# Batch 0's decays apart from the other batches', in a re-ordered Mamba-2 and low-rank-mixer kernel

## The chip, the cores and the metric

The kernel runs on one core of one Trainium2 chip. The metric is the device time of one execution in microseconds (us). Runs of the same kernel differ by about 1%: the three runs of the kernel before took 219.33, 219.85 and 221.1 us.

## What is computed

Two blocks, one behind the other. The first is a chunked state-space scan (Mamba-2 SSD) with batch 4, 8 heads, sequence 768, head dimension 32 and state dimension 16; the second is a low-rank token mixer with a channel MLP on the 256 joined channels.

```python
# first block: x (4,8,768,32), a (4,8,768), B and C (4,8,768,16)
log_a = np.log(np.clip(a, 1e-06, 1.0))
for c in range(nc):                       # chunks of 32 steps
    cum = np.cumsum(la, axis=-1)
    L = np.exp(cum[:, :, :, None] - cum[:, :, None, :]) * causal
    y_intra = ((C B^T) * L) x
    y_inter = (C state) * exp(cum)
    state = exp(sum(la)) * state + sum_j B_j x_j exp(cum[-1] - cum_j)
# second block: x (4,768,256) from the first, U (768,32), V (32,768)
h = x.transpose(0, 2, 1) @ U @ V
u = x + h.transpose(0, 2, 1)
out = u + np.maximum(u @ w_ch1, 0.0) @ w_ch2     # w_ch1 (256,1024), w_ch2 (1024,256)
```

The weights U, V, w_ch1 and w_ch2 arrive as 64-bit floats. The kernel loads them as pairs of 32-bit words and builds single-precision numbers from them on the chip.

## The kernel before

The scan works on chunks of 64 steps. A batch has 768 steps, which are three "pairs" of two blocks of 128 steps, so there are twelve pairs, k = 0 to 11, three for each batch. The kernel is written as small steps, and one long string, PLAN (lines 41 to 75), lists every step in the order in which it is issued. `follow` (line 937) reads the words of the list one by one; there is no scheduler behind it. Each engine (TensorE is PE, VectorE is DVE, ScalarE is ACT, GpSimd is POOL, SyncE is SP) works off its own share of the list in that order, and waits where an operand or a buffer is not ready. Two more strings give each product its PSUM bank (BANKS) and each temporary its place in memory (SLOTS).

At the start, outside of the list, `a` is loaded, turned by two PE products (line 358), clamped by one DVE operation for all four batches (line 360) and put through the logarithm by one ACT operation (line 364). A product of ones (`ahead`, line 312) stands on PE before and after the turning, only to keep PE at work.

The words of the list that matter here; a digit behind the letter is the pair, or the batch:

- `A` (`decays`, line 384): products of the logarithms with a fixed matrix, then ACT's exponential into F; the word's number says whether the factors of B (0) or of C (1) are made. `K` (`keep`, line 403): three products, DVE's `own` and its reduction, ACT's exponential and a POOL product give the decays that carry the state from chunk to chunk (`kept`, `own2`). Before the change, both are for all four batches at once.
- `YX`, `YB`, `YU`, `YV`, `X`, `B`, `w`: loads on SP's queue, x as `x`, B and C as `bc`, and the weights as `words`. `X`, `B` and `w` without a Y are held until the DVE operation last listed is done (`hold`, line 202). `w0` and `w1` bring the first quarter of w_ch1 in two halves, `w2` to `w4` the other three, `w5` to `w8` the quarters of w_ch2.
- `Q` and `P` (`prep`, line 481): DVE multiplies B and C by the factors F into `BC`. `V` and `T` (`turn`, line 520): PE transposes BC, ACT or DVE copies it to `T` and `Cm`.
- `g` (`gram`): 32 products for C B^T; `m` and `M` (`mask`, line 549): DVE applies the causal mask into `M`. `n` and `j` (`intra`, line 676): each half of the intra-chunk products; `j` waits for a small POOL copy (`settled`, line 617), which waits for the products of `n`. `s` (`state`): products for the states, `u` (`update`): DVE's chain of states S, then POOL's product `Sm`. `i` (`inter`): products with the carried state.
- `y`, `t`, `O`: ACT copies the result of a pair out of PSUM, PE transposes it into token order (`ytok`).
- `p`, `q`, `a` (`project`, `parted`, `added`, from line 742): the low-rank mixer. `v` (`spread`, line 893): Vs is made from V. `c`, `C` (`convert`) and `R` (`refined`): the conversion of weights, in three steps over DVE, ACT and POOL, and their split into parts for the fast product form.
- `U` and `d0.0` (`plain`, `down`): the MLP of the first half of batch 0 in full single precision; `S`, `f`, `h`, `d`: the MLP of everything else, from split operands.
- `E` (`warm`, line 349) is a fill: PE multiplies the identity by itself, n blocks of 128 columns in one product, into a bank that nobody reads. It computes nothing.

Of the kernel before, what the change touches and what calls it, by code (L numbers as in the profile page):

```python
# [14 lines left out]
WCOLS = 512  # L15
PLAIN = 1
BANKS = (
    '01720345670012367400561273334612337423057406175233406175234061752304237562137054713054762167'
    '2305417351473512603512476305143051247626241762405761357204615304712530471240653206127346126731'
    '26705706254317062705647031520312304504153761021072016325040375403')  # L20
SLOTS = (
    'abcdefghijklmnocaefbdgihmecjbldkagofhimncjekandeblmneogmfcmhjiakdbnolefhmgcadjnbeilofkhjcmdeal'
    'gibfonmkjeclhbagfidnkomlej')


NEAR = 1.0 - 2.0 ** -13
# [3 lines left out]
AF = mybir.ActivationFunctionType  # L30
ALU = mybir.AluOpType
# [7 lines left out]


PLAN = (
# [34 lines left out]


@with_exitstack
def kernel(
# [27 lines left out]
    nc = tc.nc  # L107
# [249 lines left out]
    for g in range(2):  # L357
        nc.tensor.transpose(out=la_ps[:, g], in_=a_sb[:, g], identity=ident[:R, :R])
    ahead(80)
    vector.tensor_scalar(  # L360
        out=la.rearrange("p b c h -> p b h c"),
        in0=la_ps.rearrange("p g (b h c) -> p (g b) h c", h=NH, c=NC),
        scalar1=1e-6, scalar2=1.0, op0=ALU.max, op1=ALU.min)
    nc.scalar.activation(la, la, AF.Ln)

    middle = const.tile([P, P], FP32)
    vector.tensor_tensor(out=middle, in0=low[1], in1=low[0], op=ALU.subtract)
# [16 lines left out]
    def decays(bs, tag="w", which=range(2)):  # L384

        n = bs.stop - bs.start
        for i in which:
            d = bank(tag, n * NPR * NH * 2)
            view = d.rearrange("p (g h c) -> p c g h", g=n * NPR, h=NH)
            logs = la[:, bs].rearrange("p b (q c) h -> p c (b q) h", q=NPR)  # L390
            if i == 0:
                nc.tensor.matmul(out=view, lhsT=ref, rhs=logs, start=True, stop=True,
                                 skip_group_check=True)
            for c in range(2 if i else 0):
                for t in range(2):
                    nc.tensor.matmul(
                        out=view[ts(c, H), t], lhsT=ref.rearrange("p (i t) -> p t i", t=2)[:, t],
                        rhs=logs[:, c], start=t == 0, stop=True, skip_group_check=True)
            nc.scalar.activation(
                F[:, bs, :, :, i].rearrange("p b q h c -> p (b q h) c"),  # L400
                d.rearrange("p (g c) -> p g c", c=2), AF.Exp, scale=(-1.0, 1.0)[i])
# [485 lines left out]
    def convert(c, scalar=False):  # L887

        if c not in steps:
            steps[c] = to_fp32(*weights[c], c - 2 - NQ, scalar)  # L890
        next(steps[c])
# [33 lines left out]
    def ytokens_of(k, v):  # L925
# [4 lines left out]
                 j=lambda k: intra(k, 1), y=yout, t=ytokens, Q=lambda k, c: prep(k, c, 1),  # L930
                 O=ytokens_of,
                 V=lambda k, c, v: turn(k, c, 1, "wx"[v // 2], vector if v % 2 else None))
    whole = dict(c=convert, b=lambda c: convert(c, True), C=lambda n: convert(-1), R=refined, A=lambda i: decays(every_batch, "w", [i]),
                 K=lambda n: keep(every_batch, "z"), F=fill, E=warm,
                 v=lambda n: spread())

    def follow(plan):
# [54 lines left out]
```

## Time and profile before

| | before |
|---|---|
| median of three runs | 219.85 us (219.33 to 221.1) |
| the profiled execution, its own time | 221.66 us |
| its span, first to last instruction | 219.9 us |
| mean granted TensorE clock | 0.977 |
| PE busy | 211.3 us |
| DVE, ACT, POOL busy | 150.1, 87.6, 35.4 us |
| moved by DMA | 14.58 MB |

The profile is one execution, with every instruction's start and length on each engine. "Busy" is the time in which an engine had at least one instruction in work. For PE the ends are modelled, and consecutive products overlap. A row of the timeline gives the start, the time from the first start to the last end of a group, the engine, the source line, the operation, output and inputs, the shape and the count, and in brackets the idle time ahead of it with the instruction that ended it. A single-precision product is recorded as two passes, a transpose as one. Line 182 stands for all DVE operations, since a helper records them. SPq rows are the issuing of loads and stores; the data land later. "PEclk" is the share of full speed that the clock throttle granted to PE.

### The profile page before, as it was taken

The numbers are of one execution on the slowest core, as the hardware profiler recorded it, in microseconds if no ns is written. First come the engines' busy times: TensorE is split into PE (matmuls) and PEld (weight loads), VectorE is DVE, ScalarE is ACT, GpSimd is POOL, SyncE is SP. The second block draws the span as 40 slices with busy tenths as digits, with TensorE's granted clock in tenths as the row PEclk, the third lists the DMA queues.
The fourth block names the chain that finished last, engine by engine and source line by source line (L and its number), as shares of the span: only waits on it lengthen the run. The fifth ranks groups of instructions, "written<-read, shape, count | busy, mean of one in ns | idle before, by whom it ended". The sixth has DMA issues, their size and how long they took to land.

```text
span 219.9 us, 7021 instructions
## 1 busy us (share of the span) xinstructions
PE 211.3 (96%) x3058; PEld 186.8 (85%) x3058; DVE 150.1 (68%) x314; ACT 87.6 (40%) x196; POOL 35.4 (16%) x52
## 2 busy tenths in 40 slices
PE   7879989998999999999999999999999999999994
PEld 3646756666778989999999988999999999999993
DVE  4737796787768899789653779746518776647532
ACT  2342736567574555443053531236342222323000
POOL 3011023368570740001000101200000000000000
PEclk9965999999999999999999999999999999999999
DMA  5989584678686850203210301000000000100012
GB/s 94 107 121 133 121 139 110 143 217 216 135 117 118 132 62 3 48 16 82 29 51 3 72 3 48 30 3 1 3 0 24 30 23 0 48 16 11 0 53 93
DMA packets 69663, 14.58 MB, mean 66 GB/s; under 512 B 63808, under 2 KB 67840, under 8 KB 69632
## 3 DMA queue, kind: packets, MB, share of 16 engines
q1 hardware_dynamic: 69488, 14.06, 32.6%
q8 instruction: 24, 0.39, 0.8%
q10 hardware_dynamic: 144, 0.07, 0.1%
q14 instruction: 7, 0.06, 0.1%
HBM read 10.98 MB, written 3.15 MB: 64 GB/s over the span
## 4 chain that ended last, share of the span: by engine, by line
PE 86%; DVE 6%; SPq 3%; DMA 1%; issue 1%; POOL 1%; DVEq 0%; POOLq 0%
PE x L809 38%; PE z L809 27%; PE y L694 4%; SPq L210 3%; PE y L658 3%; PE x L544 2%; PE w L504 2%; DVE words L182 2%; PE w L721 2%; PE w L140 2%; DMA bc<-in_C_dram 1%; PE w L578 1%; DVE M L182 1%; DVE S L182 1%; PE w L747 1%
## 5 line engine op out<-in xcount | busy, mean ns | idle before, releaser
L182 DVE SCALAR_TENSOR_TENSOR words<-words 128x768 fp32r<-128x768 f32 (+3 forms) x39 | 35.9, 919 | 5.1 <-PE z L809 3.4
L809 PE MATMUL x<-w,words 128*128 128x256 f32 x224 | 34.4, 284 | 0.0
L809 PE MATMUL x<-u,w 128*128 128x384 f32 x168 | 33.9, 340 | 0.0
L809 PE MATMUL z<-u,w 128*128 128x384 f32 x168 | 33.0, 340 | 0.0
L833 ACT ACTIVATE words<-x 128x384 fp32r<-128x384 f32 x28 | 13.8, 492 | 44.0 <-PE x L809 43.9
L809 PEld LDWEIGHTS x<-w,words 128*128 128x128 f32 x224 | 30.5, 190 | 0.2 <-issue 0.2
L809 PEld LDWEIGHTS z<-u,w 128*128 128x128 f32 x168 | 29.1, 188 | 0.3
L809 PEld LDWEIGHTS x<-u,w 128*128 128x128 f32 x168 | 28.8, 188 | 0.4 <-issue 0.2
L809 PE MATMUL x<-w2c,words 128*128 128x256 f32 x144 | 25.2, 305 | 0.0
L833 ACT ACTIVATE words<-z 128x384 fp32r<-128x384 f32 x28 | 13.7, 491 | 25.3 <-PE z L809 25.3
L809 PEld LDWEIGHTS x<-w2c,words 128*128 128x128 f32 x144 | 21.1, 189 | 1.1 <-issue 0.4
L182 DVE SCALAR_TENSOR_TENSOR words<-z,words 128x384 fp32r<-128x384 f32 x28 | 15.4, 551 | 9.0 <-ACT words L833 8.9
L809 PE MATMUL z<-w,words 128*128 128x256 f32 x112 | 18.4, 287 | 0.0
L182 DVE SCALAR_TENSOR_TENSOR words<-x,words 128x384 fp32r<-128x384 f32 x28 | 14.9, 551 | 4.0 <-ACT words L833 3.8
L605 POOL TENSOR_TENSOR Sm<-S,own 128x256 f32<-128x256 f32 (+1 forms) x12 | 7.2, 602 | 61.6 <-DVE S L182 61.6
L809 PEld LDWEIGHTS z<-w,words 128*128 128x128 f32 x112 | 15.7, 190 | 0.2
L694 PEld LDWEIGHTS y<-M,x 64*32 64x32 f32 x768 | 8.7, 113 | 5.9 <-POOL settled L617 2.8
L694 PE MATMUL y<-M,x 64*32 64x64 f32 x768 | 12.0, 237 | 1.5 <-POOL settled L617 1.3
L809 PE MATMUL z<-w2c,words 128*128 128x256 f32 x72 | 13.2, 307 | 0.0
L182 DVE SCALAR_TENSOR_TENSOR S<-S,kept,w 128x64 f32<-128x64 f32 x40 | 11.2, 280 | 2.6 <-PE w L504 0.5
L182 DVE TENSOR_TENSOR M<-x,causal 128x256 int32<-128x256 int32 x24 | 9.0, 416 | 5.7 <-PE z L544 4.3
L182 DVE SCALAR_TENSOR_TENSOR ytok<-x,ytok 128x256 f32<-128x256 f32 (+1 forms) x17 | 6.8, 407 | 7.3 <-PE x L809 7.3
(137 smaller groups left out, 337.3 us busy)
## 6 DMA issues: line engine op xcount, KB each, us to landing
words<-in_moe_w_ch_dram SPq DMA_DIRECT2D x7, 512.0 KB, 5.3
x<-in_x_dram SPq DMA_DIRECT2D x24, 128.0 KB, 3.2
out_dram<-ytok SPq DMA_DIRECT2D x23, 128.0 KB, 1.7
bc<-in_B_dram SPq DMA_DIRECT2D x24, 64.0 KB, 3.2
bc<-in_C_dram SPq DMA_DIRECT2D x12, 128.0 KB, 3.3
words<-in_moe_w_ch_dram SPq DMA_DIRECT2D x2, 256.0 KB, 3.0
words<-in_moe_U_dram SPq DMA_DIRECT2D x1, 192.0 KB, 3.5
words<-in_moe_V_dram SPq DMA_DIRECT2D x4, 48.0 KB, 2.5
```

The lines of the kernel that those rows point to most:

```text
L140: nc.tensor.matmul(out=t[:, :m * P].rearrange("p (m i) -> p m i", i=P), lhsT=ident, rhs=ident[:, None, :].to_broadcast([P, m, P]), start=T ...
L182: self.last = call(*args, **kwargs)
L210: op = issuer[0].dma_start(**kwargs)
L504: nc.tensor.transpose(out=tp[:, i, v], in_=s["BC"][:, i, c + v].rearrange("p h n -> p (h n)"), identity=ident)
L544: nc.tensor.matmul(out=s["g"][r][cols, c], lhsT=s["T"][rows, 0, c, cols], rhs=s["Cm"][rows, :, :, ts(2 * c + p, Q)].rearrange("r v t i -> ...
L578: nc.tensor.matmul(out=s["A"][p][ts(r, Q), v], lhsT=s["BC"][half, 0, v, 2 * r:2 * r + 2].rearrange("p h n -> p (h n)"), rhs=x_sb[k][half, ...
L605: nc.gpsimd.tensor_tensor(out=s["Sm"][:, sl], in0=s["S"][:, sl].rearrange("p i (s d) -> p i s d", s=2), in1=own2[:, b, 4 * q + sl.start:4 ...
L658: nc.tensor.matmul(out=channels(k)[r // 2][ts(r % 2, H), c, p], lhsT=own[ts(r, Q)], rhs=st[k]["T"][ts(r, Q), 1, :, ts(2 * c + p, Q)].rearr ...
L694: product = nc.tensor.matmul(out=y[n][ts(i, Q), c, p], lhsT=x_sb[k][half, c, h], rhs=s["M"][half, h // 2, c, h % 2], start=fresh(k, n, [i] ...
L721: nc.tensor.transpose(out=t[:, c, g], in_=yT[b][:, g, ts(2 * q + c, P)], identity=ident)
L809: nc.tensor.matmul(out=t, lhsT=lhsT, rhs=rhs, start=start, stop=True, skip_group_check=True)
L833: nc.scalar.activation(gs[j, m // 2][0][:, m % 2], t, AF.Relu, scale=NEAR)
```

## The change

Behind the turning of `a`, the clamp is made twice, for batch 0 and for the other three; the logarithm of batch 0 follows at once, that of the others is a word of the list (`L0`). `A` now has four words, 0 and 1 for batch 0, 2 and 3 for the others, and `K` two. F, `kept` and `own2` are written by parts; their values are the same.

The list has a new order from the first word to the last, and so have BANKS and SLOTS. The first words are shown below up to the first products of the MLP; behind them the same words follow in another order. Fills before: E1, E2, E1, E1, E2, E1 (eight blocks, the first two words `E1` and `E2` ahead of the first intra products). After: E4 as the very first word, ahead of the decays, then E2, E4, E2 (twelve blocks).

```diff
-    vector.tensor_scalar(
-        out=la.rearrange("p b c h -> p b h c"),
-        in0=la_ps.rearrange("p g (b h c) -> p (g b) h c", h=NH, c=NC),
-        scalar1=1e-6, scalar2=1.0, op0=ALU.max, op1=ALU.min)
-    nc.scalar.activation(la, la, AF.Ln)
+    first, rest = slice(0, 1), slice(1, NB)
+    for bs in (first, rest):
+        vector.tensor_scalar(
+            out=la[:, bs].rearrange("p b c h -> p b h c"),
+            in0=la_ps.rearrange("p g (b h c) -> p (g b) h c", h=NH, c=NC)[:, bs],
+            scalar1=1e-6, scalar2=1.0, op0=ALU.max, op1=ALU.min)
+
+    def logs(bs):
+
+        nc.scalar.activation(la[:, bs], la[:, bs], AF.Ln)
+
+    logs(first)
...
-    whole = dict(c=convert, b=lambda c: convert(c, True), C=lambda n: convert(-1), R=refined, A=lambda i: decays(every_batch, "w", [i]),
-                 K=lambda n: keep(every_batch, "z"), F=fill, E=warm,
+    whole = dict(c=convert, b=lambda c: convert(c, True), C=lambda n: convert(-1), R=refined, L=lambda n: logs(rest),
+                 A=lambda i: decays((first, rest)[i // 2], "w", [i % 2]),
+                 K=lambda n: keep((first, rest)[n], "z"), F=fill, E=warm,
...
 PLAN = (
-    'YX0 A0 YB0 Q0.0 YB1 A1 Q0.2 Q0.1 K0 s0 YB2 YB3 Q1.0 V0.0.0 V0.1.1 Q1.2 YU0 YX1 Q1.1 u0 '
-    'Q2.0 E1 Q2.2 g0 m0 V1.0.2 B5 M0 V1.1.2 w0 V2.0.2 E2 n0 j0 g1 YX2 YV0 m1 i0 E1 P3 E1 M1 Q2.1 c0 '
-    's1 n1 u1 c0 T3 T3 E2 V2.1.3 c1 P5 j1 y0 i1 g2 m2 w1 O0.0 s2 c1 B4 y1 T5 u2 M2 T5 g3 C0 m3 i2 '
-    'n2 E1 X3 c0 j2 M3 y2 C0 c2 t1 C0 w3 c2 O2.1 v0 p0 s3 P4 T4 u3 X4 q0 c2 w2 T4 g5 a0.0 M5 X5 c4 '
-    'w5 m5 n3 c1 U0.0.1 U0.0.0 j3 g4 i3 c4 w6 c4 y3 m4 c3 s4 U0.0.4 R0 t3 U0.0.5 c3 c3 R1 u4 a0.1 '
-    'B6 U0.0.3 M4 c6 i4 w4 n5 c6 R0 n4 w7 c6 s5 U0.0.2 j4 j5 u5 y4 i5 c7 c7 y5 t4 d0.0.1.0 R4 t5 '
+    'E4 L0 A1 YX0 A0 YB0 Q0.0 YB1 YX1 Q0.2 Q0.1 V0.0.0 Q1.0 YU0 V0.1.1 K0 Q1.1 A2 s0 g0 Q1.2 YB2 '
+    'YV0 m0 V1.0.2 M0 V1.1.2 A3 n0 j0 YX2 g1 u0 Q2.0 m1 YB3 K1 B5 i0 y0 M1 s1 n1 c0 w0 X3 E2 w1 '
+    'Q2.2 C0 Q2.1 O0.0 j1 V2.0.2 s2 u1 E4 V2.1.3 i1 y1 u2 P3 g2 m2 M2 t1 P5 T3 T3 i2 c1 n2 C0 j2 g3 '
+    'E2 m3 c0 w3 C0 y2 O2.1 c0 v0 p0 M3 c2 c2 c1 B4 s3 c2 n3 u3 q0 T5 T5 a0.0 c1 w2 c4 c4 R0 j3 '
+    'a0.1 w4 U0.0.1 U0.0.0 P4 X4 g5 i3 c3 w5 c4 T4 y3 w6 U0.0.4 X5 c3 M5 T4 U0.0.5 m5 c5 c3 R0 '
+    'U0.0.3 t3 R2 c5 c5 s4 u4 c6 g4 U0.0.2 w7 c6 m4 M4 U0.0.6 c6 U0.0.7 c7 i4 c7 R2 c7 R1 d0.0.1.0 '
...
```

More of the change, by code (lines that the diff above doesn't have):

```diff
@@ L17 @@
 BANKS = (
-    '01720345670012367400561273334612337423057406175233406175234061752304237562137054713054762167'
-    '2305417351473512603512476305143051247626241762405761357204615304712530471240653206127346126731'
-    '26705706254317062705647031520312304504153761021072016325040375403')
+    '0120203456712035462034562714570062300146035271436005271403652714032714023765021743650215074362'
+    '2615643132015647013014756201362017453625254364152734620153470623470562503465036403267015430145'
+    '6726701453762145376521037634737437437142630750736506412547342453')
 SLOTS = (
-    'abcdefghijklmnocaefbdgihmecjbldkagofhimncjekandeblmneogmfcmhjiakdbnolefhmgcadjnbeilofkhjcmdeal'
-    'gibfonmkjeclhbagfidnkomlej')
+    'abcdefghijklmnodabgcefihladjgmifnkclbadhojecdhjmfjgnmbknbiloaecdgfhmnkjliboakcgejdhflnmcobieja'
+    'gndkfhmliocbjenaghdmkofjic')
 NEAR = 1.0 - 2.0 ** -13
```

56 rows, old and new, of the table PLAN are left out of this document.

## The prediction

> **What bounds the kernel now.** I read the cores' spans first, then the page's busy table and chain by engine, then a table of stretches, and last the timeline, engine by engine, up to the first product of the mixer.
>
> ```profile
> core 0: 219.9 us, clock 0.977
> PE 211.3 (96%) x3058; PEld 186.8 (85%) x3058; DVE 150.1 (68%) x314; ACT 87.6 (40%) x196; POOL 35.4 (16%) x52
> PE 86%; DVE 6%; SPq 3%; DMA 1%; issue 1%; POOL 1%; DVEq 0%; POOLq 0%
> ```
>
> PE holds 86% of the chain that ended last. Its products are nearly the same before and after, so the change can only win where PE waits or runs slowly. The stretches say where (columns: length, then busy time of PE, PEld, DVE, ACT, POOL, then granted clock, DMA share, GB/s):
>
> ```profile
> 9.28:12.69 3.41, 2.23 (x39) 1.36 (x40) 2.84 (x10) 2.36 (x10) 0.62 (x1) 1.00 0.93 113
> 12.69:16.10 3.41, 2.98 (x98) 1.86 (x102) 0.76 (x3) 0.75 (x3) 0.18 (x1) 0.50 0.75 121
> 16.10:19.52 3.42, 3.30 (x101) 2.60 (x88) 2.62 (x9) 0.38 (x1) 0.00 (x0) 0.50 0.83 118
> 19.52:22.93 3.41, 3.35 (x69) 2.13 (x55) 1.63 (x7) 1.33 (x3) 0.79 (x2) 0.50 1.13 175
> 29.76:33.17 3.41, 2.75 (x48) 1.32 (x49) 2.96 (x9) 1.99 (x7) 0.73 (x1) 1.00 0.78 160
> 70.00:80.00 10.00, 10.00 (x166) 9.42 (x164) 9.24 (x19) 5.30 (x11) 5.84 (x6) 1.00 0.82 120
> 80.00:100.00 20.00, 20.00 (x224) 19.62 (x201) 17.63 (x34) 9.22 (x19) 0.89 (x2) 1.00 0.14 29
> ```
>
> From 70 us PE is full. The loss lies in the first 37 us, and 10.24 us of it (12.69 to 22.93) ran at half clock, after a stretch in which PE was busy 2.23 of 3.41 us. These PE rows carry the rest:
>
> ```profile
> 2.13 1.06 PE L315 MATMUL x<-ones 128*128 128x512 f32 x1
> 4.51 1.01 PE L392 MATMUL w<-la,ref 128*128 128x192 f32 x2
> 9.60 0.35 PE L544 MATMUL x<-Cm,T 32*64 32x128 f32 x2 [0.89 <-DVE BC L182]
> 10.33 0.66 PE L504 MATMUL x<-ident,BC 128*128 128x128 f32 x4
> 12.51 1.08 PE L140 MATMUL w<-ident 128*128 128x256 f32 x2
> 13.64 0.68 PE L694 MATMUL y<-M,x 64*32 64x64 f32 x32
> 14.70 0.68 PE L694 MATMUL y<-M,x 64*32 64x64 f32 x32 [0.37 <-POOL settled L617]
> 15.31 0.48 PE L544 MATMUL x<-Cm,T 32*64 32x128 f32 x2
> 17.04 1.65 PE L140 MATMUL w<-ident 128*128 128x128 f32 x4
> 18.74 0.68 PE L578 MATMUL w<-x,BC 64*32 64x64 f32 x32
> 19.88 1.11 PE L504 MATMUL w<-ident,BC 128*128 128x128 f32 x4
> 20.79 1.06 PE L140 MATMUL w<-ident 128*128 128x256 f32 x2
> 22.53 0.61 PE L694 MATMUL y<-M,x 64*32 64x64 f32 x32
> 29.18 0.46 PE L694 MATMUL y<-M,x 64*32 64x64 f32 x32
> 31.53 0.35 PE L901 MATMUL y<-Vn,ident 32*32 32x192 f32 x2 [0.52 <-ACT Vn L895]
> 37.18 1.53 PE L809 MATMUL z<-yT,w1f 128*128 128x384 f32 x4
> ```
>
> The same four transposes cost 0.66 at full clock and 1.11 at half; 32 intra products 0.46 and 0.68. PE was busy 3.30 of 3.42 us in 16.10:19.52 and the clock still did not return, while 19.52:22.93 (3.35) brought it back. What differs is work on the whole 128x128 array: 1.65 of fills in the first; 1.11 and 1.06 and two more transposes in the second. I therefore count whole-array work, not busy time.
>
> **The change part by part.** DVE and the loads decide the early steps:
>
> ```profile
> 6.03 0.29 DVE L182 TENSOR_TENSOR BC<-bc,F 128x128 f32<-128x128 f32 x1 [1.29 <-DMA bc<-in_B_dram]
> 7.41 0.52 DVE L182 TENSOR_TENSOR own<-z,mine 128x352 f32<-128x352 f32 x1
> 8.60 0.60 DVE L182 TENSOR_SCALAR Cm<-w,slot 128x128 f32<-128x128 f32 x2
> 10.16 0.91 DVE L182 SCALAR_TENSOR_TENSOR S<-S,kept,w 128x64 f32<-128x64 f32 x3
> 11.63 0.49 DVE L182 TENSOR_TENSOR BC<-bc,F 128x256 f32<-128x256 f32 x1 [0.36 <-DMA bc<-in_C_dram]
> 12.04 0.74 DVE L182 TENSOR_TENSOR M<-x,causal 128x256 int32<-128x256 int32 x2
> 16.52 0.76 DVE L182 TENSOR_TENSOR M<-x,causal 128x256 int32<-128x256 int32 x2 [3.08 <-PE z L544]
> 13.92 1.17 SPq L210 DMA_DIRECT2D x<-in_x_dram  x2
> 20.58 3.00 SPq L210 DMA_DIRECT2D words<-in_moe_V_dram  x4
> words<-in_moe_w_ch_dram SPq DMA_DIRECT2D x7, 512.0 KB, 5.3
> x<-in_x_dram SPq DMA_DIRECT2D x24, 128.0 KB, 3.2
> 41.93 0.76 DVE L182 TENSOR_SCALAR words<-words 128x512 f32<-128x512 f32 x2
> 42.72 0.69 DVE L182 SCALAR_TENSOR_TENSOR words<-words 128x512 int32<-128x512 int32 x1
> 43.55 1.30 POOL L447 TENSOR_TENSOR w1f<-words 128x512 int32<-128x512 int32 x1 [2.04 <-DVE words L182]
> ```
>
> 1. The fill ahead of the decays (E4, two passes of 512 columns) stands on PE just where the decays started, at 4.51. A pass of this width took 1.06 alone at 2.13; two cost at most 2.1, at full clock half as much. I take 1.6: decays at 6.1. The split makes the first decays 24 columns a block wide where they were 96, so both with their exponentials need about 1.0 where 1.5 went by (4.51 to 6.03). The first BC product comes at 7.1 instead of 6.03: 1.1 lost.
> 2. That loss is covered by DVE's new order. Before, own and its reduction (0.52 each, all batches) stood ahead of Cm at 8.60; now Cm comes first, again at 8.6, and own has a quarter of the elements. The first gram starts at 9.5 (before 9.60): 0.
> 3. Before the first masks (12.04) DVE did three S updates (0.91) and two BC products of the third pair, the second waiting for a load until 11.63. Now only one BC product (0.49) and the small own stand there: masks at 10.5, 1.5 won.
> 4. The way from masks to the first intra products (12.04 to 13.64) held the fill of 1.08; it is gone. Intra at 11.3 and 12.7 (before 13.64, 14.70), second gram at 13.2, where it was 15.31: 2.1 won.
> 5. The second pair's intra waited for the mask at 16.52, for 1.65 of fills, and for the state products of 18.74, whose x was issued at 13.92 to 15.09 and takes 3.2 to land. SP now issues that x ninth instead of seventeenth, about 7.3, landing near 11. In return U and V go ahead of the third and fourth pairs' B and C: the third pair's, issued at 7.25 before, now at about 9, land by 14, and DVE reaches them at 13: at most 1 on a product that nothing early waits for, taken as 0. The rest of the batches' kept sums (three quarters of the columns) now cost about 0.7 of PE here and 0.85 of DVE. The intra of the second pair comes at 15.9; before it followed the state products, at about 19.2: 3.2 won.
> 6. Its second half stood at 22.53, behind four transposes and a fill. Now a fill of 256 and four output transposes with ACT's copy stand there: 18.1. As many transposes lie ahead of it in both orders: 4.4 won.
> 7. The next fill (512) stands ahead of the last two transposes of pair 3, which its Cm (0.60) and gram need: 0.85 at full clock. Last intra of batch 0 at 25.1 (before 29.18): 4.1 won.
> 8. V is issued about 11 to 13 instead of 20.58 to 23.58, so Vn (31.53) no longer waits for it, but its subtraction stands behind copies on DVE. First mixer product at 34.0 (before 37.18). By then one gram (about 0.7) and a little transposing are still owed, an intra half and two added products are done early, net 0.4: 2.8 won.
> 9. The load for the second quarter of w1 is held until the first added sums (about 34.0). With 5.3 to land (row of 512.0 KB), 0.76 and 0.69 on DVE and POOL's add of 1.30, PE may stand up to 1.4 at U0.0.3; nothing if it lands in 4. I take 0.4, as little else loads then.
> 10. Clock. Whole-array work is thin between 6.1 and 16: no fill stands there. I expect one stretch of 3.4 at half clock instead of three, as the 1.1 of kept products and the second gram fill the next one; 0.4 on the path (bounds 0 and 1.2).
> 11. Eight more small products, two clamps for one, and three more ACT operations lie in steps 1 to 5; beside PE they cost nothing, and if that cover goes (DVE in step 5) at most 0.4.
>
> Past 40 us every product is the same, in another order, on a full PE: 0 taken, bounds 0.7 either way. Sum: 2.8 - 0.4 - 0.4 = 2.0 won. The profiled execution took 221.66 with a span of 219.9; the median of the runs shown is 219.85, so I take the 2.0 off the median: 217.9.
>
> **The rivals.** (a) The clock falls early and stays down as long as now. For it: the 24-column decays leave PE idle from about 6.7 to 7.5, and a busy share of 2.23 in 3.41 was enough to fall. Price: the path of steps 3 to 6 at half clock, in rows 1.11-0.66 for each four transposes (two on the path), 0.68-0.46 for each of five groups, 0.6 for the second fill, about 2.6 in all; then 220.5 less 0.7 for the shorter waits, 219.8, no change. The Trainium skill, "TensorE: Matmul & The Clock Gate", Part 1, says that the gate judges free-running windows of about 3.4 us, unrelated to the start of the kernel; the stretches of 3.41 in this trace agree, and by this rule (a) and the forecast can alternate from run to run.
>
> (b) Slower: the clock falls once more at about 30. In 29.76:33.17 PE was busy only 2.75 with narrow products and the clock held; in the new order the fill lies 2 us ahead of those products and the stretch may hold less. The half clock would then meet the dense mixer and cost half its length. The one fall that the trace shows lasted three stretches: 5.1, and 217.9 + 5.1 = 223.0. It decides from two stretches on (3.4 against the 2.0 won); one stretch (1.7) would only eat the gain.
>
> (c) The start is won and given back: DVE is busy 9.24 of 10 in 70:80 and 17.63 of 20 in 80:100, only 3.1 idle in 30, and the refined weights it makes there must come 2.0 earlier. Against it: DVE too starts earlier, and had spare time before. If 1.2 is given back, 219.1.
>
> **How the numbers follow.** About 1% (2.2 us) is what a measurement of this kernel can tell from no change. Forecast 0.42 (217.9, its own range 216.9 to 219.1 by the bounds of steps 9 and 10; 0.18 of it below 217.65). The same without steps 9 and 10, with a clock that never falls: 219.85 - 2.8 = 217.1, 0.17. Then (a) 0.18, (b) 0.15, (c) 0.08. Faster by over 1%: 0.18 + 0.17 = 0.35. Slower by over 1% (above 222.05): 0.13 of (b) and 0.04 of (a), where the fill of 512 in step 7 still meets half clock: 0.17. The rest, 0.48, is within 1%. The range 216.4 to 221.4 lowers the best case by the 0.7 of the last part, goes up to the one or two stretches of (b), and leaves out about a fifth.
>
> **What would show it.** Right: first mask near 10.5, last intra of batch 0 near 25, first product of w1f near 34, no or one stretch at 0.50, PE full from there with the same 180 us behind it. Wrong: three stretches at 0.50 again (a), a second fall after 28 (b), PE waiting for POOL's w1f near 41 (step 9), or PE gaps between 60 and 100 with DVE as releaser (c).

## The result and the profile after

| | before | after |
|---|---|---|
| median on the chip | 219.8 us (219.33 to 221.1) | 223.5 us (223.36 to 223.62) |
| ratio to the kernel before, 95% interval | | 1.0148 (1.0104 to 1.0192) |
| the same, measured again | | 223.7 us, 1.0133 (1.0071 to 1.0194) |
| the profiled execution, its own time | 221.66 us | 223.56 us |
| its first product of w1f | 37.18 us | 37.00 us |

The change costs about 1.4%; I had forecast 217.9. Medians here are over all timed executions of a kernel, ratios go to the kernel before on the same chip. The ratios leave disturbed executions out, so they can differ a little from those of the medians. The span of after:

```profile
core 0: 221.9 us, clock 0.992
```

Its page, busy times and the chain by engine:

```profile
PE 211.9 (95%) x3070; PEld 185.5 (84%) x3070; DVE 151.5 (68%) x317; ACT 88.5 (40%) x200; POOL 36.2 (16%) x52
PE 86%; DVE 6%; POOL 2%; issue 2%; DMA 2%; ACT 1%; DVEq 0%; POOLq 0%
```

The stretches of after, with the columns of the prediction:

```profile
6.75:10.16 3.41, 2.77 (x56) 2.13 (x54) 2.21 (x9) 1.75 (x7) 0.00 (x0) 1.00 0.88 117
10.16:13.58 3.42, 3.42 (x84) 2.43 (x76) 2.52 (x9) 1.97 (x9) 0.29 (x1) 0.50 1.05 161
13.58:16.99 3.41, 3.04 (x140) 2.46 (x134) 2.61 (x8) 0.25 (x2) 0.80 (x2) 1.00 0.58 103
45.00:55.00 10.00, 10.00 (x211) 6.48 (x209) 9.54 (x19) 6.05 (x12) 5.75 (x6) 1.00 0.63 183
55.00:65.00 10.00, 9.03 (x149) 7.54 (x134) 7.24 (x11) 5.18 (x11) 6.05 (x7) 1.00 0.76 130
80.00:100.00 20.00, 20.00 (x268) 19.36 (x268) 17.57 (x33) 10.43 (x22) 1.18 (x2) 1.00 0.36 58
```

In this execution the clock did as forecast: one stretch at half clock (10.16 to 13.58) where the profile of before had three. PE is full in 80:100, as before; in 55:65 it is not. The rows of the start:

```profile
4.53 1.91 PE L140 MATMUL w<-ident 128*128 128x512 f32 x2
6.37 0.58 PE L403 MATMUL w<-la,ref 128*64 128x24 f32 x8
7.58 1.03 DVE L182 TENSOR_TENSOR BC<-bc,F 128x128 f32<-128x128 f32 x4 [2.72 <-ACT F L406]
11.35 0.76 DVE L182 TENSOR_TENSOR M<-x,causal 128x256 int32<-128x256 int32 x2 [0.75 <-PE z L551]
12.03 0.75 DVE L182 TENSOR_TENSOR M<-z,causal 128x256 int32<-128x256 int32 x2
12.96 0.68 PE L701 MATMUL y<-M,x 64*32 64x64 f32 x32
16.85 0.39 PE L701 MATMUL y<-M,x 64*32 64x64 f32 x8
17.49 0.65 PE L701 MATMUL y<-M,x 64*32 64x64 f32 x24 [0.25 <-DVE M L182]
20.16 0.46 PE L701 MATMUL y<-M,x 64*32 64x64 f32 x32 [0.67 <-ACT ytok L736]
21.29 1.13 PE L140 MATMUL w<-ident 128*128 128x512 f32 x2
22.95 0.61 DVE L182 TENSOR_SCALAR Cm<-x,slot 128x128 f32<-128x128 f32 x2 [2.86 <-PE x L511]
27.95 0.46 PE L701 MATMUL y<-M,x 64*32 64x64 f32 x32 [0.56 <-POOL settled L624]
37.00 1.45 PE L816 MATMUL z<-yT,w1f 128*128 128x384 f32 x4
```

The kernel is ahead of the profile of before by 2.4 us at the second half of pair 1 (20.16 against 22.53), by 1.2 at the last intra product of batch 0, and by 0.2 at the first product of w1f. So even against that profile the start gained nothing by 37 us. One place behind it stands out:

```profile
54.33 1.61 POOL L454 TENSOR_TENSOR w2c<-words 128x512 int32<-128x512 int32 x1 [1.15 <-issue]
55.88 0.18 POOL L624 COPY settled<-slot 128x1 f32<-128x1 f32 x1
56.12 0.86 PE L701 MATMUL y<-M,x 64*32 64x64 f32 x64 [0.97 <-POOL settled L624]
```

`settled` takes 0.18 us, but on POOL's queue it stands behind the add of a weight conversion that started late, and PE waits for it.

### The profile page after: what moved, and what is told of

Its sections match the earlier page's. It is cut to its first block, busy times and chain, and to the rows that moved or that the text cites. A ratio compares the mean times of both kernels' runs of the same rounds, so it can differ in the third digit from the quotient of the medians.

```text
span 221.9 us, 7062 instructions
## 1 busy us (share of the span) xinstructions
PE 211.9 (95%) x3070; PEld 185.5 (84%) x3070; DVE 151.5 (68%) x317; ACT 88.5 (40%) x200; POOL 36.2 (16%) x52
## 4 chain that ended last, share of the span: by engine, by line
PE 86%; DVE 6%; POOL 2%; issue 2%; DMA 2%; ACT 1%; DVEq 0%; POOLq 0%
PE x L816 36%; PE z L816 25%; PE y L701 4%; PE x L551 3%; DVE words L182 2%; PE y L665 2%; PE w L511 2%; PE w L140 2%; DMA words<-in_moe_w_ch_dram 2%; PE w L728 2%; PE x L315 1%; PE w L585 1%; PE w L754 1%; PE w L772 1%; PE x L511 1%
## 5 line engine op out<-in xcount | busy, mean ns | idle before, releaser
L182 DVE SCALAR_TENSOR_TENSOR words<-words 128x768 fp32r<-128x768 f32 (+3 forms) x39 | 34.1, 876 | 3.1 <-PE x L816 1.4
L816 PE MATMUL z<-u,w 128*128 128x384 f32 x168 | 33.8, 342 | 0.0
L816 PE MATMUL x<-u,w 128*128 128x384 f32 x168 | 33.4, 339 | 0.0
L816 PEld LDWEIGHTS z<-u,w 128*128 128x128 f32 x168 | 28.6, 188 | 0.5 <-issue 0.2
L816 PE MATMUL x<-w2c,words 128*128 128x256 f32 x144 | 26.0, 307 | 0.0
L816 PE MATMUL z<-w,words 128*128 128x256 f32 x112 | 17.6, 287 | 0.0
L612 POOL TENSOR_TENSOR Sm<-S,own 128x256 f32<-128x256 f32 (+1 forms) x12 | 8.7, 722 | 40.9 <-DVE S L182 40.7
L182 DVE TENSOR_TENSOR BC<-bc,F 128x512 f32<-128x512 f32 (+2 forms) x18 | 10.8, 620 | 6.6 <-DMA bc<-in_B_dram 3.6
L719 ACT COPY yT<-y 128x256 f32<-128x256 f32 x24 | 7.7, 375 | 14.2 <-PE y L701 9.3
```

Source lines behind the costliest of these rows:

```text
L182: self.last = call(*args, **kwargs)
L612: nc.gpsimd.tensor_tensor(out=s["Sm"][:, sl], in0=s["S"][:, sl].rearrange("p i (s d) -> p i s d", s=2), in1=own2[:, b, 4 * q + sl.start:4 ...
L719: nc.scalar.copy(out=yT[b][:, n, ts(q, 2 * P)], in_=st[k]["y"][n].rearrange("p c v i -> p (c v i)"))
L816: nc.tensor.matmul(out=t, lhsT=lhsT, rhs=rhs, start=start, stop=True, skip_group_check=True)
```

## The experiments

My theories at this point: (1) the base of my forecast was an untypical execution; (2) `settled` behind the add costs 1 us; (3) the fills and the load `w2` hold the start back; (4) the split costs something by itself. The rival to all: the new order as a whole is worse, in no one place.

### The kernel before and after once more

> The kernel before, once more, for a second profile: of 22 executions so far those with a mean granted clock of 0.977 to 0.983 took 221.4 to 222.0, those near 0.992 took 220.7 to 221.3, and those from 0.997 up 218.7 to 220.3. The first profile was of the slowest kind (0.977, three stretches at half clock). Theory A, the half clock lies on the path of the start: if this execution has a clock of 0.997 or more, its first product of the MLP comes near 35.2 instead of 37.18, so that the changed kernel's start (37.00, with one such stretch) is later than an ordinary execution of the kernel before, and not level with it. Rival B: the start is the same 37 and the 2 us lie elsewhere.

Measured: 219.22 us. Its span:

```profile
core 0: 217.5 us, clock 1.000
```

Two of its stretches:

```profile
10.16:13.58 3.42, 2.83 (x63) 1.47 (x50) 2.50 (x9) 2.48 (x9) 1.05 (x2) 1.00 0.90 104
13.58:16.99 3.41, 2.81 (x108) 2.11 (x108) 2.21 (x7) 0.38 (x1) 0.00 (x0) 1.00 0.99 163
```

Its first intra product, the second half of pair 1, the last of batch 0, and the first product of w1f:

```profile
12.55 0.65 PE L694 MATMUL y<-M,x 64*32 64x64 f32 x32
...
19.61 0.46 PE L694 MATMUL y<-M,x 64*32 64x64 f32 x32
...
26.75 0.46 PE L694 MATMUL y<-M,x 64*32 64x64 f32 x32
...
34.73 1.53 PE L809 MATMUL z<-yT,w1f 128*128 128x384 f32 x4
```

Theory A holds. Without half clock the old order reaches its first product of w1f at 34.73, 2.45 earlier than in the profile that I had read, and ends 2.4 earlier. Such executions are the commoner kind: of 120 timed executions of the kernel before, 66 had a granted clock of 0.997 or more (median 219.28 us), 54 a lower one (median 221.28). After is behind this execution at every one of the four rows (12.96, 20.16, 27.95, 37.00), at the last by 2.3.

> The changed kernel once more. Theory A, its order draws one stretch at half clock in nearly every execution: clock 0.990 to 0.992 and 223.4 to 223.6 again; an execution without that stretch (0.998 and up) would take 222.3 to 222.8. Rival B: the clock hardly moves its time, 223.5 at any clock.

Measured: 223.89, 224.28 and 223.56 us at a clock of 0.990 to 0.992, 222.71 at 0.998. With the first four, seven of eight executions of after have the stretch at half clock (median 223.6); the one without is 3.4 above the kernel before at the same clock. So the clock explains part of the difference, and most of it lies elsewhere. The start shows it too: e3_add_behind_j4 below has the list of after up to 54 us, and its profile has no half clock at all behind 7.31 us; its first product of w1f stands at 36.37, still 1.6 behind b0_before_again.

How much was lost where is an estimate of mine: I gave each product a fixed time by its kind, the same in all kernels, and subtracted the sum of those begun from the time. What is left is waiting, fills and half clock (us):

```
up to                    40 us   65 us   200 us
before, profile shown     19.1    20.2     23.0
b0_before_again           16.5    17.7     20.6
after                     19.1    21.5     25.0
f1_unsplit_three_edits    16.3    17.5     20.8
```

Against b0_before_again, after loses 2.6 by 40 us, 1.2 more by 65 (2.4 against 1.2) and 0.6 more by 200. Other times for the kinds move each of these by half a us or so, so the last of them isn't firm.

### The add behind j4

```diff
-... i4 c7 R2 c7 R1 d0.0.1.0 d0.0.0.0 n4 B6 n5 s5 j4 u5 j5 ...
+... i4 c7 R2 R1 d0.0.1.0 d0.0.0.0 n4 B6 n5 s5 j4 c7 u5 j5 ...
```

> The changed kernel with one word moved: the POOL add of the weight conversion c7 stands behind the second intra half of pair 4 (j4), no longer ahead of it, so that the small copy 'settled' is not behind that add on POOL. Theory A: the wait of 0.97 us at 55 goes, and the add (1.6) is done before its weights are needed: 222.5. Rival B: the conversions of w_ch2 on DVE and POOL are what limits PE here, and the wait comes back a little later, at the first product with that weight: 223.5, same lag at 65 us.

Measured: 222.25 us, ratio 1.0107 (1.007 to 1.0144). POOL and PE there:

```profile
54.49 0.18 POOL L624 COPY settled<-slot 128x1 f32<-128x1 f32 x1 [1.78 <-PE y L701]
54.63 1.29 POOL L454 TENSOR_TENSOR w2c<-words 128x512 int32<-128x512 int32 x1
...
54.73 0.86 PE L701 MATMUL y<-M,x 64*32 64x64 f32 x64
55.52 1.13 PE L816 MATMUL x<-w2c,words 128*128 128x256 f32 x4
```

Theory A: the products of 56.12 come at 54.73, with no wait ahead of them, and the add still ends before the weight is needed. How much of it reaches the end is less certain. The medians differ by 1.3 us and the ratios by 0.9, and their intervals overlap. But e3_add_behind_j4 kept a clock of 0.997 or more in 6 of 12 executions and after in one of eight, though the lists are the same up to 54 us, so the seven of eight were in part chance and the medians mix this in. At equal clock the edit wins 0.4 (223.2 over six executions with a lower clock, against 223.6 over seven of after) or 0.9 (221.8 over six at 0.997 or more, against the single 222.7).

The same edit in the kernel before:

```diff
-... R0 n4 w7 c6 s5 U0.0.2 j4 j5 u5 ...
+... R0 n4 w7 s5 U0.0.2 j4 c6 j5 u5 ...
```

> The kernel before with one word moved: the POOL add of the weight conversion c6 (48.55, 1.61) behind the second intra half of pair 4, so that 'settled' (50.11) doesn't wait for it. Theory A, the same wait as in the changed kernel, shorter: 0.5 to 0.9 won, 218.9 to 219.2. Rival B: no change, 219.7, since the conversions limit PE there and the wait comes back at the first product with that weight.

Measured: 219.48 us, ratio 0.9968 (0.9928 to 1.0008); at a clock of 0.997 or more 218.78, where the kernel before has 219.28. The sign and size fit theory A, but the interval still touches 1.

In e6_add_behind_and_act the first word of each of four conversions is the variant whose first step runs on ACT:

```diff
-... c6 ... c7 ... c8 ... c9 ...
+... b6 ... b7 ... b8 ... b9 ...
```

> The changed kernel with the add behind j4 as in e3_add_behind_j4, and with the first step of the conversions c6 to c9 (one of three operations that DVE makes for each, 0.42 to 0.76) on ACT, which is 60 per cent busy there while DVE is 95 per cent busy. Theory A, DVE's queue of conversions holds PE back between 40 and 60, which is where earlier starts are given back: 0.5 to 1.0 less than the 222.25 of e3_add_behind_j4, so 221.3 to 221.8. Rival B, the loads or PE's own stream set it: 222.25. Rival C, ACT's copies of the scan are delayed: 222.8.

Measured: 222.52 us, 1.0092 (1.0052 to 1.0132): rival B, no gain over e3_add_behind_j4. DVE was 95% busy in 45:55 of after, and taking work from it there bought nothing.

### The fills and the load

```diff
-E4 L0 A1 ...        (e1_no_first_fill)     -... s2 u1 E4 V2.1.3 ...   (e2_small_third_fill)
+L0 A1 ...                                  +... s2 u1 E1 V2.1.3 ...
```

> The changed kernel without its first fill (the E4 ahead of the decays, 4.53 to 6.44 in its trace); nothing else differs. Theory A, the fills are paid on the path and the start is set by the chain from decays to masks: the decays come at about 4.9 instead of 6.37, the first BC product near 6.1 (7.58), and about 1.0 is won: 222.5. Rival B, this fill holds the clock: without it the clock falls a stretch earlier or stays low for two or three stretches, and the time is 223.5 to 225. Rival C, whatever the first 10 us win is lost again in the waits for DVE between 20 and 37: 223.5, with the first product of the MLP still at 37.0.

Measured: 224.02 us, 1.0205 (1.0152 to 1.0257): theory A is wrong, nothing is won at the end without the first fill. The start did win 0.85: in the profile the first product of w1f comes at 36.15 instead of 37.00, and PE then waits 0.41 for w1f at 44.13. Rival B's reason isn't borne out either: the clock fell in 3 of 6 executions, and those that kept it were no faster (223.3 to 225.8).

> The changed kernel with its third fill cut from four blocks to one (the second E4, 21.29 to 22.4, ahead of the last two transposes of pair 2). Theory A: DVE stands idle 2.86 us until 22.95 behind those transposes, so three quarters of the 1.13 us are on the path: 0.8 won, 222.7. Rival B: the stretch of 3.4 us then holds too little whole-array work, the clock falls near 24 and the time is 224.5 to 226. Rival C: the time between 23 and 37 is set elsewhere (the V load, UV, the conversions), no change, 223.5.

Measured: 223.16 us, 1.0136 (1.0093 to 1.0179): well under half of what A expected. In its profile the first product of w1f comes at 34.60, near the 34.0 that I had forecast, and yet the end gains little. A part of why, in its rows:

```profile
4.39 1.02 PE L140 MATMUL w<-ident 128*128 128x512 f32 x2
...
34.60 1.45 PE L816 MATMUL z<-yT,w1f 128*128 128x384 f32 x4
42.69 1.56 PE L816 MATMUL z<-yT,w1f 128*128 128x384 f32 x4 [0.42 <-POOL w1f L454]
...
39.71 0.76 DVE L182 TENSOR_SCALAR words<-words 128x512 f32<-128x512 f32 x2 [1.63 <-DMA words<-in_moe_w_ch_dram]
```

The first row was not edited: the same fill took 1.91 in after and 1.02 here, because the clock rose earlier in this execution (the trace has full clock from 4.32 us here and from 6.75 in after), so a good part of the 34.60 is chance. The other rows show the start running into the weights: DVE waits 1.63 for `w2`, which is held until the first added sums, and PE for their conversion. In a0_after_again the unedited kernel, whose first product of w1f stands at 36.82, meets the same wait:

```profile
42.04 0.76 DVE L182 TENSOR_SCALAR words<-words 128x512 f32<-128x512 f32 x2 [1.73 <-DMA words<-in_moe_w_ch_dram]
...
45.01 1.56 PE L816 MATMUL z<-yT,w1f 128*128 128x384 f32 x4 [0.43 <-POOL w1f L454]
```

So the next two kernels cut the fill without and with an earlier load:

```diff
-... s2 u1 E4 V2.1.3 ...          -... c0 v0 p0 ... a0.0 c1 w2 c4 ...
+... s2 u1 E1 V2.1.3 ...          +... c0 w2 v0 p0 ... a0.0 c1 c4 ...
```

> The changed kernel with the add behind j4 (as in e3_add_behind_j4) and the third fill cut from four blocks to one (as in e2_small_third_fill). Theory A, two separate losses, the 1.0 us wait for 'settled' and 0.85 us of fill: their gains add, 221.2 in the median, 220.4 in executions with a granted clock of 0.997 or more. Rival B, the time of the fill is given back before 50 us, because the load of the second quarter of w_ch1 is held until the first added sums and PE waits for it sooner (in the trace of e2_small_third_fill DVE waits 1.63 us for those words at 39.7 and PE 0.42 at 42.7): 222.0.

> As e7_add_and_small_fill, and the load of the second quarter of w_ch1 (w2) is listed ahead of the spreading of V, some 4 us earlier, instead of behind the first added sums. Theory A, that load is what gives the shorter start back between 40 and 45: DVE's wait of 1.6 for the words goes, and 0.5 to 0.8 is won against e7_add_and_small_fill. Rival B, the loads of pair 4's B and C now stand behind it on SP's queue and the wait moves to them: no difference to e7_add_and_small_fill.

> As e8_and_w2_early (220.84), but with the third fill at its four blocks again: the changed kernel with the add behind j4 and the load w2 early. Theory A, with the load early the fill of 1.13 is on the path: 0.5 to 0.9 more than e8_and_w2_early, 221.3 to 221.7. Rival B, the third fill lies beside DVE's chain, and all of the 1.5 between e7_add_and_small_fill and e8_and_w2_early is the load: 220.6 to 221.0.

Measured, all with the add behind j4:

| third fill | load late | load early |
|---|---|---|
| four blocks | 222.25, ratio 1.0107 (e3_add_behind_j4) | 221.98, ratio 1.0106 (1.0063 to 1.0148) |
| one block | 222.38, ratio 1.0087 (1.0056 to 1.0118) | 220.84, ratio 1.0016 (0.9981 to 1.0052) |

By these medians neither edit alone wins anything clear, and both together 1.4 us. But the four kernels differ in their clock: 0.997 or more in 6 of 12 executions of e3_add_behind_j4, none of 6 of e11_w2_early_full_fill, 2 of 11 of e7_add_and_small_fill and 6 of 12 of e8_and_w2_early. The medians of the executions with a lower clock alone:

| third fill | load late | load early |
|---|---|---|
| four blocks | 223.2 (6 executions) | 222.0 (6) |
| one block | 222.4 (9) | 221.5 (6) |

At equal clock the early load wins 1.2 with the full fill and 0.9 with the small one, and the small fill 0.8 and 0.4; of so few executions the last is within the scatter. Both together win 1.7, and 1.7 at a clock of 0.997 or more too (221.8 and 220.1). (The kernels ran on three chips, on which the kernel before took 221.2 to 221.4 at a lower clock.) So rival B of e7_add_and_small_fill, that the load gives back what the small fill wins, is not shown, though its number came out; the two gains roughly add. Theory A of e8_and_w2_early holds: DVE's wait of 1.46 us for these words in e7_add_and_small_fill is gone, and so is PE's of 0.4 for w1f. The spans of the two profiles, both with one stretch at half clock, differ by 0.9 (220.8 and 219.9). The rest of the 1.5 between their medians is the clock.

### The split

First the split alone, in the old list:

```diff
-YX0 A0 YB0 Q0.0 YB1 A1 Q0.2 ... V0.1.1 Q1.2 ... V1.1.2 w0 ... i0 E1 P3
+YX0 A0 YB0 Q0.0 YB1 A1 L0 Q0.2 ... V0.1.1 A2 Q1.2 ... V1.1.2 A3 w0 ... i0 K1 E1 P3
```

> The kernel before, in its own order with its own fills, with the split alone: clamp, logarithm, decays and kept sums of batch 0 first, those of the other batches put into the old list (their logarithm behind the second decays, their decays behind the transposes of pair 0 and 1, their kept sums behind the first carried products). Theory A, the split itself shortens the start: decays and kept sums of 24 columns a block, masks about 0.5 earlier, 0.3 to 0.8 won against before: 219.0 to 219.5. Rival B: the split costs, since 0.7 of PE and 0.85 of DVE are added while both are on the path: 220.3 to 220.8. Rival C: no change, 219.8, since the new order and the fills are what changed the time.

```diff
-... Q2.0 E1 Q2.2 ... V2.0.2 E2 n0 ... i0 E1 P3     (e10_split_in_fill_places, beside L0 as above)
+... Q2.0 A2 Q2.2 ... V2.0.2 A3 E1 n0 ... i0 K1 P3
```

> The kernel before with the split alone, as in e4_split_alone, but with the other batches' decays and kept sums in the places of fills: their first decays instead of the first E1, the second ahead of E2 (cut to E1) in a bank of their own, their kept sums instead of the third fill. In e4_split_alone PE waited 1.46 at 12.43 for the masks, because I had given the second decays a bank that the masks still read. Theory A, the split costs nothing where it takes the place of fills: 219.0 to 219.6 at a granted clock of 0.997 or more, as the kernel before. Rival B, the split lengthens the start wherever it stands: 220.5 or more at that clock. Rival C, with three fills fewer the clock falls more often.

Measured: 222.72 us, 1.0102 (1.0058 to 1.0146), and 223.69 us, 1.0103 (1.0053 to 1.0152); at a clock of 0.997 or more 222.5 and 221.7, against 219.28. Both are slower by much more than I thought, but they do not measure the split alone: each carries waits of the places that I chose. In e10_split_in_fill_places PE waits 0.9 for ACT's F and 0.5 for `own`; one of e4_split_alone, 1.46 for the masks:

```profile
12.43 0.75 PE L403 MATMUL w<-la,ref 128*64 128x72 f32 x8 [1.46 <-DVE M L182]
```

So I went the other way and undid the split in the new list, with clamp, logarithm, `A` and `K` as before, first alone and then with the three edits.

```diff
-E4 L0 A1 ... K0 Q1.1 A2 s0 ... V1.1.2 A3 n0 ... YB3 K1 B5 ...
+E4 A1 ... K0 Q1.1 s0 ... V1.1.2 n0 ... YB3 B5 ...
```

> The changed kernel's list with the split undone: clamp, logarithm, decays and kept sums for all four batches at once, at the places where those of batch 0 stand; the four words for the other batches (L0, A2, A3, K1) are left out. Theory A, the split is worth about nothing by itself, the new order and its fills made the time: 223.2 to 223.8. Rival B, the split wins in the start (decays of 96 columns a block and own of four times the size stand ahead of the first masks): without it 224.2 to 224.8. Rival C, the split costs (0.7 of PE and 0.85 of DVE for the rest, a second time through ACT): without it 222.5 to 223.0.

> The changed kernel's list with the split undone (as in e9_new_order_unsplit) and with the three edits of e8_and_w2_early: the add behind j4, the third fill of one block, the load w2 early. Theory A, four separate losses: the split (about 1.0 at a granted clock of 0.997 or more, 222.7 to 221.7), the wait for 'settled' (1.0), the fill (0.85) and the late load (0.5): together 219.2 to 219.6 at that clock. Rival B, the gains overlap, since the split's cost and the others lie on the same path before 45 us: 220.2 to 220.8, no better than e8_and_w2_early at that clock (220.1). Rival C, with the small third fill the clock falls more often than in e9_new_order_unsplit (2 of 12 executions), and the median is above 220.5.

Measured: e9_new_order_unsplit 221.73 us, 1.0072 (1.0037 to 1.0107), and f1_unsplit_three_edits 219.64 us, 0.9991 (0.9966 to 1.0016). Rival C of the first holds, by more than it expected: without the split the median is 1.8 lower, and at a clock of 0.997 or more 1.0 (221.7 over ten executions against the single 222.7 of after). With the three edits in both kernels the split costs 0.5 at that clock (f1_unsplit_three_edits 219.64 over twelve, e8_and_w2_early 220.10 over six). The starts of two profiles without half clock, from e3_add_behind_j4 (split) and e9_new_order_unsplit, agree:

```profile
36.37 1.45 PE L816 MATMUL z<-yT,w1f 128*128 128x384 f32 x4
```

```profile
34.99 1.45 PE L809 MATMUL z<-yT,w1f 128*128 128x384 f32 x4
```

Of these 1.4 us, 0.6 is the first fill, which took 1.91 in the one and 1.35 in the other execution; 0.8 is left for the split. The rest is how often the clock falls. With the split it fell in 7 of 8 executions of after, 6 of 12 of e8_and_w2_early, and in 43 of 67 of all kernels with the new list and its first fill; without it in 2 of 12 of e9_new_order_unsplit and none of 12 of f1_unsplit_three_edits. Undoing the split and three edits take back the whole 1.5% of the medians; at a clock of 0.997 or more f1_unsplit_three_edits is still 0.4 above the kernel before on the same chip (219.25). Rows of f1_unsplit_three_edits, with a span of 217.7 at full clock:

```profile
4.43 1.10 PE L140 MATMUL w<-ident 128*128 128x512 f32 x2
...
34.33 1.45 PE L809 MATMUL z<-yT,w1f 128*128 128x384 f32 x4
```

The first fill taken out of this list, and put into that of the kernel before:

```diff
-E4 A1 YX0 ...      (f5_unsplit_no_first_fill)     -YX0 A0 YB0 ...       (f4_before_first_fill_add)
+A1 YX0 ...                                        +E4 YX0 A0 YB0 ...
```

> As f1_unsplit_three_edits (219.64, eleven of eleven executions at a granted clock of 0.997 or more), without the first fill. Theory A, the fill ahead of the decays delays the start by the 1.0 to 1.9 that it takes, of which about half reaches the end: 218.9 to 219.2, better than the kernel before at any clock. Rival B, the first fill is what keeps the clock up: executions with half clock come back and the median is 220.3 or more. Rival C, its time is slack: 219.6.

> The kernel before with the fill of four blocks ahead of its decays and the add of c6 behind j4 (as in e5_before_add_behind_j4). Theory A, whole-array work ahead of 10 us decides whether the clock falls: with this fill nearly every execution keeps 0.997 or more (in the kernel before fewer than half did, in e9_new_order_unsplit, which has this fill and the unsplit decays, 10 of 12), at a price of 0.2 to 0.4: 219.2 to 219.4 in nearly every execution, median below the 219.48 of e5_before_add_behind_j4. Rival B, the fill's 1.3 us lie on the path: 220.2. Rival C, the clock falls as often as before whatever stands there.

Measured: f5_unsplit_no_first_fill 220.73 us, 1.0022 (0.9983 to 1.0062); f4_before_first_fill_add 219.15 us, 1.0004 (0.9971 to 1.0037). Rival B of the first: without the first fill the clock fell in 5 of 12 executions, with it in none, and at full clock nothing was won. In the old list the same fill did not keep the clock: 4 of 12 fell; nor did it in the split list, where 3 of 6 fell without it (e1_no_first_fill) and 43 of 67 with it. So whole-array work early on helps in one order and is not enough in others; what decides is not settled. Neither kernel is shown to beat the kernel before.

### The old order behind 64 us

```diff
-... p1 P8 R3 B11 d0.0.2.3 S0.1 d0.0.1.3 q1 u6 d0.0.0.3 X7 ...
+... p1 P8 R3 B11 d0.0.2.3 T6 q1 X8 R6 B10 P7 a1.0 R7 T7 T7 d0.0.1.3 ...
```

> As e8_and_w2_early up to the word S0.1 (about 64 us), and behind it the rest of the words in the order of the kernel before, with banks and places given anew (each product gets the bank that has been free longest). Theory A, the new order itself costs about 0.5 behind 65 us (time less the streaming of products grows by 2.9 between 65 and 200 us in the kernel before, by 3.4 to 3.5 in every kernel with the new list): 0.5 less than the 220.84 of e8_and_w2_early, 220.3. Rival B, the difference is in how products of different shapes follow each other anyway, or in waits that the other head brings: no difference. Rival C, the banks given anew bring waits of their own: slower than 221.

> f1_unsplit_three_edits with the old order behind S0.1, as in f2_edits_old_tail: what is left of the change is the new order of the first 64 us without its losses. Theory A: 218.8 to 219.3 at a granted clock of 0.997 or more, which is the kernel before (219.3) or slightly better. Rival B, the new order of the start is itself longer than the old one: 219.8 or more at that clock.

Measured: 225.7 us, 1.0256 (1.0197 to 1.0316), and 224.62 us, 1.0224 (1.0191 to 1.0257): rival C of the first. The seam made waits of its own. DVE in f2_edits_old_tail waits for a load, and PE for DVE's `ps` behind it (the timeline, then the waits of PE from 62 to 75 us):

```profile
64.94 0.69 DVE L182 TENSOR_TENSOR BC<-bc,F 128x512 f32<-128x512 f32 x1 [3.13 <-DMA bc<-in_B_dram]
```

```profile
PE x L782 <- DVE ps L182: 1.7, 1, 1.7
```

They say nothing on the order behind 64 us. Whether it costs the 0.4 to 0.6 that the table above puts there stays open.

## Why the prediction was wrong, by its steps

Three terms failed above all: the base, from which half clock was won back that the median did not have; the split, put at nothing beside PE (step 11); and the order past 40 us, put at nothing. Step 4 counted a fill on a path where it was not.

**The base, where it failed first.** "The profiled execution took 221.66 ... so I take the 2.0 off the median": the 2.0 was worked out against an execution with three stretches at half clock, and taken off a median of executions that mostly have none. Of the 2.8 that step 8 puts at the first product of w1f, 2.45 were that half clock (37.18 against 34.73 in b0_before_again). My 34.0, had it come, was 0.7 better than that start: 0.7 off the median, 219.2, and no change by my own bound. The 1.8 us by which the profile's own time lay above the median stood in the text, and I did not ask what they were.

**Steps 1 and 2.** BC at 7.58 (forecast 7.1): the fill took 1.91, not the 1.6 I took, and decays with exponentials 1.2, not 1.0. The gram came at 10.14 (9.5).

**Steps 3 and 4.** Masks at 11.35 (10.5), intra at 12.96 (11.3). Step 4 failed: I counted the fill of before (12.51 to 13.59) as on the path to the first intra product. It lay beside the second pair of masks, which that product needs as well. The row of before that I left out:

```profile
12.71 0.74 DVE L182 TENSOR_TENSOR M<-z,causal 128x256 int32<-128x256 int32 x2
```

These masks end at 13.45, and the product came at 13.64; in after they end at 12.78, and it comes at 12.96. Taking the fill away could win 0.2 at most, not 1.08: from the first mask to the product it took 1.60 before and 1.61 after, where I had taken 0.8.

**Steps 5 to 8.** Step 5: the first products of the second pair at 16.85 (15.9), so it won more than I took, and the 1.7 of step 4 shrank to 1.0. Step 6: 20.16 (18.1), 1.1 more lost; PE waits 0.25 for the masks and 0.67 for ACT's `ytok`, and the step has neither. Step 7: 27.95 (25.1), 0.8 more; the fill took 1.13 (0.85 forecast) while DVE stood idle 2.86 for the two transposes behind it. Step 8: 37.00 (34.0), hardly more. What the fill of step 7 costs at the end is 0.8 or 0.4 at equal clock (the second table of the fills).

**Step 9.** Right in mechanism and size, though not in every execution: in the profile of after PE does not wait there, in a0_after_again it waits 0.43 for w1f. By the early load the whole path through it is worth 0.9 to 1.2 at equal clock.

**Step 10.** In the profile shown it is right: one stretch instead of three. But after had such a stretch in seven of eight executions, and 19 of 32 together with e3_add_behind_j4 and e6_add_behind_and_act, whose lists are the same to beyond 37 us; the kernel before had any in 54 of 120. So there was nothing to win here. The price was too low as well: executions of e3_add_behind_j4 with a lower clock took 1.4 longer than the others (223.2 against 221.8), not 0.4.

**Step 11.** Wrong: the split, taken as free beside PE, costs 0.5 at equal clock, and the clock falls in 43 of 67 executions with it and 2 of 24 without. That narrow decays leave PE too little work ahead of 10 us would fit, but the mechanism is argued, not shown.

**"Past 40 us ... 0 taken, bounds 0.7."** By the estimate above it was 1.2 between 40 and 65, of which PE's wait for `settled` is 0.97 (e3_add_behind_j4), and about 0.6 behind it, which stays unexplained. I had read this wait in its old place as small change, and did not look at what stands ahead of `settled` on POOL's queue in the new list.

**The rivals.** (b)'s 223.0 is close to the time, but for another reason: the clock never fell after 13.58. (c) had the kind of mechanism, a start that is given back where other work does not come earlier, but not the place (40 to 45 by a load, not 70 to 100 by DVE).

## What to carry to other kernels

Before a gain is taken off a median, ask how the profiled execution differs from the median one, above all in its granted clock: a loss that only the profiled execution has cannot be won. When a list is reordered, check for each tiny operation on a shared queue (here `settled`) what now stands ahead of it, and for each load held on an event whether an earlier start would meet it. A fill or an operation counts as on the path only if nothing else that the next step needs ends as late. And variants are to be compared among executions of the same clock: by their medians the small fill and the early load seemed to need each other, at equal clock each wins something by itself.

## What the runs showed of the hardware

The same fill ahead of the decays took 1.91 us in after and 1.02 in e2_small_third_fill, which are the same up to 20 us: the record of the clock has full speed from 6.75 us in the first trace and from 4.32 in the second. The Trainium skill, "TensorE: Matmul & The Clock Gate", Part 1, has the windows free-running, so that the transition depends on where in a window the first product falls; the two records agree.

Whether the clock falls again hangs on the same thing. Nine profiles share the list of after up to 20 us. In six of them full clock began between 6.40 and 6.87 us, and in each it fell one stretch of 3.41 us later. In the other three it began at 4.32, 5.31 and 7.31, and none fell there; the one from 5.31 fell at 18.96. So it can differ from execution to execution, with where the stretches lie.

The clock fell after 6.75:10.16 of after, in which PE was busy 2.77 of 3.41 us. The same Part 1 gives an idle window as what throttles the array; by these rows a window four fifths busy with mostly narrow products was enough, and the measurement decides. The busy share alone does not tell: the clock held through 7.31:10.73 of e3_add_behind_j4 with PE busy 2.78, and through 16.99:20.40 of after with 2.42.
